# The overflow branch at the beginning of the experts, and one set of transposes ahead of two matmul groups

## The chip, the cores and the metric

The kernel runs on one core of a Trainium2 chip. The time is device microseconds (us) of one launch; lower is better. The engines of the core are TensorE (PE, with its weight loads as PEld), VectorE (DVE), ScalarE (ACT), GpSimd (POOL) and SyncE (SP). Each takes its own instructions in the order in which the program wrote them, and waits on semaphores that other engines and transfers raise.

## The reference

A chain of three stages over 1536 tokens with 512 features: a linear attention with decay in blocks, a gated layer, and a mixture of eight experts, each token going to one of them. The experts' stage, cut to what matters here (`x` is what the gated layer gave; `capacity` is 384):

```
logits = x @ w_gate
expert_idx = np.argmax(logits, axis=1)
gate_w = softmax(logits)[np.arange(N), expert_idx]
for i in range(N):                      # tokens of each expert, in order
    e = expert_idx[i]
    if counts[e] < capacity:
        disp[e, counts[e]] = x[i]
        pos[i] = counts[e]; counts[e] += 1; keep[i] = True
h = np.maximum(np.einsum('ecd,edf->ecf', disp, w1), 0.0)
y = np.einsum('ecf,efd->ecd', h, w2)
out[i] = gate_w[i] * y[expert_idx[i], pos[i]]   # where keep[i], else 0
```

## The kernel before

Matmuls take each fp32 operand as two parts, high and low (`whi`/`wlo`, `xdh`/`xdl`, `hh`/`hl`), and do three products for one (`mm3`, lines 295 to 297, and line 787). The low part is made on DVE from the original less the high part that ACT wrote.

The order of all work is written by hand (`manual_schedule`): each engine gets its instructions as the code calls for them. Background work (the loading and splitting of weights by `feed` and `run_bg`) is called in small pieces between the matmul groups. The loads go out on SP's queue (line 82, `st<-e1i` and `st<-e2i`), the gathers and scatters by row index on POOL's (lines 708 and 718).

**The stage before the experts.** `x2_half(blk, cs, hooks)` computes one block of 128 tokens and one half of the features: 8 steps `fb` of three matmuls (lines 295 to 297). `hooks` names functions to call after a step; steps are numbered 0 to 7. `half_b` computes the second half with the gate's logits and starts `route`, which finds each token's expert and its place there, and adds to `csum`, whose sum over the partitions is the number of tokens of each expert. `half_a` computes the first half, and `rows_a` writes it to `xa_d` in device memory (`rowa`, line 637, on ACT's queue). The second halves lie in `xb_d`.

**The gathers.** `gathers(e, half)` brings the rows of expert `e` from `xa_d` (half 0, tiles `xga`) or `xb_d` (half 1, tiles `xgb`) into one of two sets of buffers, in two chunks of 128 rows. `table` issues those of half 1 for experts 0 and 1. Those of half 0 can start only when the last block of `xa_d` is stored.

**The experts.** `dispatch(e, half)` transposes the gathered rows by four PE instructions (line 757), then ACT writes `xdh` (line 769) and DVE `xdl` (line 770). `mm1(e, pr, ks)` does the first layer for the pair `pr` of 128 hidden units each: for the half of the features in `ks`, `(2, 3)` being half 1 and `(0, 1)` half 0, 12 matmuls of 128x256 (line 787). At the beginning only half 1 is there, so all four pairs of expert 0 and two of expert 1 start with `(2, 3)`, six groups of 12, before half 0 of expert 0 is used. Then comes the loop over the experts, with the second layer (`mm3` with `hh`/`hl`) and the scatter of each result.

**More than 256 rows.** The main path holds two chunks, so 256 rows of an expert. `overflow()` does what lies beyond: all engines load the largest count (`cmax`, line 833) into a register and branch on it (`tc.If`, line 834). With these inputs no expert has more than 256 rows, so the body is jumped over at run time. The counts are made by one matmul of `ones` with `csum` (line 817) and a maximum on DVE (line 819). In the program the branch stands in the loop:

```
for e in range(NE):
    if nch > 2 and e == OVER:      # OVER = 7
        overflow()
```

Of the kernel before, what the change touches and what calls it, by code (L numbers as in the profile page):

```python
# [12 lines left out]
I32 = mybir.dt.int32  # L13
AF = mybir.ActivationFunctionType
ALU = mybir.AluOpType
AX = mybir.AxisListType
PSUM = bass.MemoryType.PSUM

P = 128
# [4 lines left out]
NE = 8  # L24
NC = 6
NBLK = NT // P
# [5 lines left out]
NST = 4  # L32
NW = (2, 1, 1, 1, 1, 1, 1, 1)
HOOK = 6
OVER = 7
LOADS = (1, 2, 2, 2, 2, 2, 2, 0)
TICKS = ((0, 0, 0, 0), (0, 0, 0, 1)) + ((1, 0, 0, 1),) * 6 + ((0, 0, 1, 0),)
XBW = 265
# [3 lines left out]
def tile_moe_chain(ctx, tc, cap, qk, kv, w12, w3i, woi, wgi, e1i, e2i, c32, c16, zero, out):  # L42
    nc = tc.nc
    nch = min(-(-cap // P), NBLK)
# [6 lines left out]
    def pool(name, bufs=1, **kw):  # L51
        return tc.tile_pool(name=name, bufs=bufs, reuse_waits="tile", **kw)

    const = ctx.enter_context(pool("const"))
# [9 lines left out]
    def bank():  # L64
        return ps.tile([P, 512], F32, tag="b", name="bank")
# [140 lines left out]
    def run_bg(n=1):  # L206
        for _ in range(n):
            feed.tick()
# [70 lines left out]
    csum = const.tile([P, NE], F16, name="csum")  # L279
# [14 lines left out]
    def mm3(acc, wh, wl, rh, rl, first, last):  # L294
        nc.tensor.matmul(acc, wh, rl, start=first, stop=False)  # L295
        nc.tensor.matmul(acc, wh, rh, start=False, stop=False)  # L296
        nc.tensor.matmul(acc, wl, rh, start=False, stop=last)  # L297
# [248 lines left out]
    ones = c16_sb[:, 128:256]  # L546
# [24 lines left out]
    def x2_half(blk, cs, hooks={}):  # L571
        g, tb = divmod(blk, 3)
        ts = slice(tb * P, (tb + 1) * P)
        acc = bank()[:, 0 : cs.stop - cs.start]
        for fb in range(8):
            gh, gl = gts[g, fb]
            mm3(acc, gh[:, ts], gl[:, ts], wxh[:, fb, cs], wxl[:, fb, cs], fb == 0, fb == 7)
            if fb in hooks:
                hooks[fb]()
        return acc  # L580
# [53 lines left out]
    def rows_a(blk, acc):  # L634
        row = p2.tile([P, 256], F32, tag="rowa", name="rowa")
        nc.scalar.copy(row, acc)
        nc.scalar.dma_start(xa_d[blk * P : (blk + 1) * P, :], row)
# [5 lines left out]
    def advance():  # L643
        for r in list(routing):
            if next(r, 0) == 0:
                routing.remove(r)

    def half_b(blk, hooks={}):
        acc = x2_half(blk, slice(256, 520), hooks)
        if not hooks:  # L650
            advance()
        routing.append(route(blk, acc))
        next(routing[-1])
        if not hooks:
            run_bg(1)

    def half_a(blk, hooks={}):
        acc = x2_half(blk, slice(0, 256), hooks)
        if not hooks:
            advance()  # L660
        rows_a(blk, acc)
        run_bg(1)
# [64 lines left out]
    def gathers(e, half):  # L727
        for s in range(nmain):
            gather(xg[e % 2][s][half], (xa_d, xb_d)[half], s * NE + e)
# [15 lines left out]
    def dispatch(e, half, apart=False):  # L745
        if e not in xd:
            xd[e] = (
                p3.tile([P, 4, nt], F32R, tag="xdh", name="xdh"),
                p3.tile([P, 4, nt], F32R, tag="xdl", name="xdl"),
                p3.tile([P, nmain], F32, tag="gate", name="gate"),  # L750
            )
        xh, xl, gt = xd[e]
        tp = psi.tile([P, 512], F32, tag="i", name="tp") if half else bank()
        tps = [tp[:, 0:nt], bank()[:, 0:nt] if apart else tp[:, nt : 2 * nt]]
        for kk in range(2):
            for s in range(nmain):
                nc.tensor.transpose(
                    tps[kk][:, s * P : (s + 1) * P],
                    xg[e % 2][s][half][:, kk * P : (kk + 1) * P],
                    ident,  # L760
                )
        k = 2 * half
        if apart:
            parts = [(xh[:, k + n, :], xl[:, k + n, :], tps[n]) for n in range(2)]
        else:
            tp = tp[:, 0 : 2 * nt].rearrange("p (k t) -> p k t", k=2)
            parts = [(xh[:, k : k + 2, :], xl[:, k : k + 2, :], tp)]
        for h, lo, src in parts:
            nc.scalar.copy(h, src)
            nc.vector.tensor_tensor(lo, src, h.bitcast(F32), op=ALU.subtract)  # L770
        if half:
            for s in range(nmain):
                nc.vector.tensor_copy(gt[:, s : s + 1], xg[e % 2][s][1][:, 264:265])

    def mm1(e, pr, ks):
        xh, xl, _ = xd[e]
        it = e1_it[2 * e + pr // 2]
        feed.need(it, pieces=2 * (pr % 2) + 2)
        if ks[0] == 2:
            accs[e, pr] = bank()[:, 0 : 2 * nt]  # L780
        acc = accs[e, pr]
        for m in range(2):
            hi, lo = (it.by_fb(part, (2 * pr + m) % 4) for part in (it.hi, it.lo))
            o = acc[:, m * nt : (m + 1) * nt]
            for k in ks:
                for w, x in ((hi, xl), (hi, xh), (lo, xh)):
                    nc.tensor.matmul(  # L787
                        o,
                        w[:, k, :],
                        x[:, k, :],  # L790
                        start=m == 0 and k == 2 and x is xl,
                        stop=m == 1 and k == 1 and w is lo,
                        skip_group_check=True,
                    )
        if ks[-1] == 1:
            hh = p3h.tile([P, 2, nt], F32R, tag="hh", name="hh")
            hl = p3h.tile([P, 2, nt], F32R, tag="hl", name="hl")
            acc = accs.pop((e, pr)).rearrange("p (m t) -> p m t", m=2)
            nc.scalar.activation(hh, acc, AF.Relu)  # L799
            nc.vector.scalar_tensor_tensor(  # L800
                hl, acc, 0.0, hh.bitcast(F32), op0=ALU.max, op1=ALU.subtract
            )
            hts[pr] = (hh, hl)
            it.free = pr % 2 == 1
        run_bg(2 if ks[-1] == 1 else 1)

    half_b(NBLK - 3, {8: advance})
    half_b(NBLK - 2, {4: advance})
    half_b(NBLK - 1, {4: advance})
    half_a(NBLK - 3, {3: advance, 6: advance, 7: table})  # L810
    half_a(NBLK - 2, {8: advance})
    acc = x2_half(NBLK - 1, slice(0, 256), {HOOK: lambda: dispatch(0, 1, apart=True)})
    rows_a(NBLK - 1, acc)
    gathers(0, 0)
    gathers(1, 0)
    cnt = bank()[:, 0:NE]
    nc.tensor.matmul(cnt, ones, csum, start=True, stop=True)
    cmax = const.tile([P, 1], I32, name="cmax")
    nc.vector.tensor_reduce(cmax, cnt, axis=AX.X, op=ALU.max)

    late.close()
    p3h = ctx.enter_context(pool("p3h", 6, side="right"))
    hts = {}
    for pr in range(4):
        mm1(0, pr, (2, 3))
        if pr == 1:
            dispatch(1, 1)
    mm1(1, 0, (2, 3))
    dispatch(0, 0)
    mm1(1, 1, (2, 3))  # L830

    def overflow():
        nmax = nc.values_load(cmax[0:1, 0:1], min_val=0, max_val=NT)  # L833
# [50 lines left out]
                    scatter(y, col)  # L884

    ov = ctx.enter_context(pool("ov", side="right")) if nch > 2 else None
    for e in range(NE):
        if nch > 2 and e == OVER:
            overflow()
        for pr in range(4):  # L890
            mm1(e, pr, (0, 1) if (e, pr) in accs else (2, 3, 0, 1))
        gt = xd.pop(e)[2]
        if e + 1 < NE:
            if e:
                dispatch(e + 1, 1)
            dispatch(e + 1, 0)
        if e + 2 < NE:
            gathers(e + 2, 1)
            gathers(e + 2, 0)
        for s in range(nmain):  # L900
            acc = bank()
            ss = slice(s * P, (s + 1) * P)
            for fb in range(8):
                it = e2_it[2 * e + fb // 4]
                feed.need(it)
                mm3(
                    acc,
                    hts[fb // 2][0][:, fb % 2, ss],
                    hts[fb // 2][1][:, fb % 2, ss],
                    it.view(it.hi)[:, fb % 4, :],  # L910
                    it.view(it.lo)[:, fb % 4, :],
                    fb == 0,
                    fb == 7,
                )
                it.free = s == nmain - 1 and fb % 4 == 3
                if fb % 2:
                    run_bg(1)
            y = p3.tile([P, DM], F32, tag="y", name="y", bufs=3)
            cut = DM if (e, s) != (NE - 1, nmain - 1) else DM // 2
            nc.scalar.activation(y[:, 0:cut], acc[:, 0:cut], AF.Copy, scale=gt[:, s : s + 1])  # L920
            if cut < DM:
                nc.vector.tensor_scalar(
                    y[:, cut:], acc[:, cut:], gt[:, s : s + 1], None, op0=ALU.mult
                )
            scatter(y, s * NE + e)
# [69 lines left out]
```

## Time and profile before

| | us |
|---|---|
| median of 3 runs | 513.52 |
| lowest and highest | 513.02, 513.99 |
| profiled execution | 516.84 |
| its span in the profile | 514.8 |
| mean granted clock of PE in it, share of full speed | 0.997 |

The rows of the profile are of one execution, and their times count from the start of its span. The profiled execution's own time (516.84) holds its span and 2.0 us that lie outside it. It is 3.3 us above the median of the runs that were not profiled.

### The profile page before, as it was taken

Reading aid. Unit: us, or ns where it says so; the run is one execution under the profiler, and the core shown is the slowest. Engines: PE = TensorE matmul, PEld = TensorE weight load, DVE = VectorE, ACT = ScalarE, POOL = GpSimd, SP = SyncE. Lnnn points to the kernel's source line nnn. Section 1 sums busy time; section 2 is a strip of 40 time slices with the busy share of each in tenths; the row PEclk is TensorE's granted clock in tenths of the full one; section 3 lists DMA queues with packets and bytes.
Section 4 is the critical chain, followed back from the end, with each engine's and each line's share of the span. In section 5 each row is a group of like instructions: output and inputs, shape, how many; then the busy total and the mean of one; then the engine's idle time right before and its main releaser. Section 6 shows DMA issues by size and latency. Waiting matters only on the chain. (4 is left out here: it accounts for less than half of the span.)

```text
span 514.8 us, 9557 instructions
## 1 busy us (share of the span) xinstructions
PE 498.6 (97%) x3805; PEld 468.7 (91%) x3805; DVE 264.9 (51%) x576; ACT 242.9 (47%) x485; POOL 128.7 (25%) x124
## 2 busy tenths in 40 slices
PE   8999999999999999999999998899999999999993
PEld 4888999999999999999999998789989898989892
DVE  5998875668332223222332563468383746547420
ACT  2697997789311221122112424457464746546310
POOL 4365664545100000000020005405414040410101
PEclk9999999999999999999999999999999999999998
DMA  8999565557801000100010224486666666574200
GB/s 325 413 410 375 155 227 204 189 187 247 320 26 41 1 0 23 43 1 0 23 43 0 88 69 157 162 299 219 214 213 211 224 224 228 177 250 171 83 2 34
DMA packets 24529, 80.80 MB, mean 157 GB/s; under 512 B 3642, under 2 KB 5692, under 8 KB 24480
## 3 DMA queue, kind: packets, MB, share of 16 engines
q1 hardware_dynamic: 18976, 70.35, 38.4%
q0 software_dynamic: 3344, 7.85, 4.8%
q10 hardware_dynamic: 2160, 1.94, 1.1%
q8 instruction: 32, 0.52, 0.4%
q14 instruction: 17, 0.14, 0.1%
HBM read 74.84 MB, written 10.54 MB: 166 GB/s over the span
## 5 line engine op out<-in xcount | busy, mean ns | idle before, releaser
L97 DVE TENSOR_TENSOR wlo<-st,whi 128x512 fp32r<-128x512 f32 x128 | 82.0, 684 | 16.7 <-ACT whi L95 16.7
L295 PE MATMUL bank<-xtl,whi 128*128 128x384 f32 x256 | 87.1, 340 | 0.0
L297 PE MATMUL bank<-xth,wlo 128*128 128x384 f32 x256 | 86.4, 337 | 0.0
L296 PE MATMUL bank<-xth,whi 128*128 128x384 f32 x256 | 85.8, 335 | 0.0
L95 ACT CAST whi<-st 128x512 fp32r<-128x512 f32 x128 | 73.1, 621 | 16.2 <-PE bank L297 10.7
L787 PE MATMUL bank<-xdl,whi 128*128 128x256 f32 x256 | 72.6, 283 | 4.7 <-issue 2.5
L787 PE MATMUL bank<-xdh,whi 128*128 128x256 f32 x256 | 72.2, 282 | 0.0
L787 PE MATMUL bank<-xdh,wlo 128*128 128x256 f32 x256 | 72.1, 282 | 0.0
L143 POOL TENSOR_TENSOR wlo<-t,whi 128x512 fp32r<-128x512 f32 x40 | 51.9, 1298 | 52.1 <-ACT whi L142 46.5
L295 PE MATMUL bank<-wxl,gh 128*128 128x264 f32 (+1 forms) x192 | 55.9, 291 | 0.0
L296 PE MATMUL bank<-wxh,gh 128*128 128x264 f32 (+1 forms) x192 | 54.1, 282 | 0.0
L297 PE MATMUL bank<-wxh,gl 128*128 128x264 f32 (+1 forms) x192 | 54.1, 282 | 0.0
L787 PEld LDWEIGHTS bank<-xdl,whi 128*128 128x128 f32 x256 | 48.4, 189 | 5.6 <-issue 2.7
L564 DVE TENSOR_TENSOR a_sb<-bank,a_sb 128x384 f32<-128x384 f32 x32 | 17.8, 557 | 66.9 <-PE bank L297 66.3
L295 PE MATMUL bank<-wlo,hh 128*128 128x512 f32 x128 | 51.1, 399 | 0.0
L297 PE MATMUL bank<-whi,hl 128*128 128x512 f32 x128 | 50.4, 394 | 0.0
L718 POOL DMA_INDIRECT out_dram<-y,idx x16 | 16.6, 1038 | 134.2 <-ACT y L920 101.1
L296 PE MATMUL bank<-whi,hh 128*128 128x512 f32 x128 | 50.0, 391 | 0.0
L800 DVE SCALAR_TENSOR_TENSOR hl<-bank,hh 128x512 fp32r<-128x512 f32 x32 | 22.1, 690 | 53.3 <-ACT hh L799 45.5
L787 PEld LDWEIGHTS bank<-xdh,whi 128*128 128x128 f32 x256 | 48.3, 189 | 0.3
L787 PEld LDWEIGHTS bank<-xdh,wlo 128*128 128x128 f32 x256 | 48.4, 189 | 0.0
L295 PEld LDWEIGHTS bank<-xtl,whi 128*128 128x128 f32 x256 | 48.1, 188 | 0.0
(109 smaller groups left out, 1006.1 us busy)
## 6 DMA issues: line engine op xcount, KB each, us to landing
st<-e1i SPq DMA_DIRECT2D x32, 512.0 KB
st<-e2i SPq DMA_DIRECT2D x32, 512.0 KB
st<-w3i SPq DMA_DIRECT2D x16, 512.0 KB
st<-w SPq DMA_DIRECT2D x16, 512.0 KB
tqk<-qk SPq DMA_DIRECT2D x8, 768.0 KB
tkv<-kv SPq DMA_DIRECT2D x8, 768.0 KB
st<-woi SPq DMA_DIRECT2D x8, 512.0 KB
out_dram<-zero SPq DMA_DIRECT2D x1, 3072.0 KB
```

The source lines that it names most:

```text
L95: nc.scalar.copy(h, s)
L97: nc.vector.tensor_tensor(lo, s, h.bitcast(F32), op=ALU.subtract)
L143: nc.gpsimd.tensor_tensor(lo, t, h.bitcast(F32), op=ALU.subtract)
L295: nc.tensor.matmul(acc, wh, rl, start=first, stop=False)
L296: nc.tensor.matmul(acc, wh, rh, start=False, stop=False)
L297: nc.tensor.matmul(acc, wl, rh, start=False, stop=last)
L564: nc.vector.tensor_tensor(a_sb, acc, a_sb, op=ALU.mult)
L718: nc.gpsimd.indirect_dma_start(out=out, out_offset=bass.IndirectOffsetOnAxis(ap=idx[:, col : col + 1], axis=0), in_=src, in_offset=None, b ...
L787: nc.tensor.matmul(o, w[:, k, :], x[:, k, :], start=m == 0 and k == 2 and x is xl, stop=m == 1 and k == 1 and w is lo, skip_group_check=True,)
L800: nc.vector.scalar_tensor_tensor(hl, acc, 0.0, hh.bitcast(F32), op0=ALU.max, op1=ALU.subtract)
```

## The change

`count`, the matmul and the maximum that give `cmax`, becomes a function and is called as a hook after step 2 of the first half of block 10 (it stood behind the gathers of `xga`; the hook `{8: advance}` that it replaces is never called, since the steps end at 7). `overflow()` is called once, before the gathers of `xga` and the first expert matmuls, and no longer in the loop. `dispatch(0, 0)`, the transposes of expert 0's first half, stands ahead of `mm1(1, 0, (2, 3))` and no longer behind it. Nothing else is changed; from there on, line numbers of the change are 1 less in the functions above and 7 to 9 less in `count` and `overflow`.

```
-OVER = 7
...
+    cmax = const.tile([P, 1], I32, name="cmax")
+
+    def count():
+        cnt = bank()[:, 0:NE]
+        nc.tensor.matmul(cnt, ones, csum, start=True, stop=True)
+        nc.vector.tensor_reduce(cmax, cnt, axis=AX.X, op=ALU.max)
+
...
-    half_a(NBLK - 2, {8: advance})
+    half_a(NBLK - 2, {2: count})
     acc = x2_half(NBLK - 1, slice(0, 256), {HOOK: lambda: dispatch(0, 1, apart=True)})
     rows_a(NBLK - 1, acc)
-    gathers(0, 0)
-    gathers(1, 0)
-    cnt = bank()[:, 0:NE]
-    nc.tensor.matmul(cnt, ones, csum, start=True, stop=True)
-    cmax = const.tile([P, 1], I32, name="cmax")
-    nc.vector.tensor_reduce(cmax, cnt, axis=AX.X, op=ALU.max)
-
     late.close()
     p3h = ctx.enter_context(pool("p3h", 6, side="right"))
-    hts = {}
-    for pr in range(4):
-        mm1(0, pr, (2, 3))
-        if pr == 1:
-            dispatch(1, 1)
-    mm1(1, 0, (2, 3))
-    dispatch(0, 0)
-    mm1(1, 1, (2, 3))
...
     ov = ctx.enter_context(pool("ov", side="right")) if nch > 2 else None
+    if nch > 2:
+        overflow()
+    gathers(0, 0)
+    gathers(1, 0)
+    hts = {}
+    for pr in range(4):
+        mm1(0, pr, (2, 3))
+        if pr == 1:
+            dispatch(1, 1)
+    dispatch(0, 0)
+    mm1(1, 0, (2, 3))
+    mm1(1, 1, (2, 3))
     for e in range(NE):
-        if nch > 2 and e == OVER:
-            overflow()
         for pr in range(4):
             mm1(e, pr, (0, 1) if (e, pr) in accs else (2, 3, 0, 1))
```

How the instructions stand on the engines, first PE between the stage before and the first expert matmul. Before:

```order
L295 MATMUL bank<-wxl,gh 128x256
L296 MATMUL bank<-wxh,gh 128x256
L297 MATMUL bank<-wxh,gl 128x256
L817 LDWEIGHTS c_sb
L817 MATMUL bank<-csum,c_sb 128x8
L787 MATMUL bank<-xdl,whi 128x256 [waits DVE_49]
L787 MATMUL bank<-xdh,whi 128x256 [waits Activation_49]
```

The count matmul is the one of line 817 (`c_sb` holds `ones`); the expert's first matmul waits for DVE's `xdl`. The same place of PE in the change:

```order
L294 MATMUL bank<-wxl,gh 128x256
L295 MATMUL bank<-wxh,gh 128x256
L296 MATMUL bank<-wxh,gl 128x256
L824 TENSOR_LOAD cmax [waits DVE_49]
L825 COMPARE_AND_BRANCH
...
L825 UNCONDITIONAL_BRANCH
L825 UNCONDITIONAL_BRANCH [waits PE_49]
L786 MATMUL bank<-xdl,whi 128x256 [waits DVE_49,PE_49]
```

In the place of the count matmul stand the load of `cmax` and the branch, whose jumped-over body is left out here; the wait of the expert's first matmul for PE itself is new. The count matmul stands further up, in the stream of block 10.

PE at the transposes of expert 0's first half (`xga00` and `xga01` are their two chunks; `bank_3947` and `bank_3971` are the results of `mm1(1, 0)` and `mm1(1, 1)`, 12 matmuls each). Before:

```order
L787 MATMUL bank_3947<-xdh_3901,whi_3771 128x256
L787 MATMUL bank_3947<-xdh_3901,wlo_3772 128x256
L757 MATMUL bank_3964<-c32_sb_79,xga00_3532 128x128
L757 MATMUL bank_3964<-c32_sb_79,xga01_3534 128x128
L757 MATMUL bank_3964<-c32_sb_79,xga00_3532 128x128
L757 MATMUL bank_3964<-c32_sb_79,xga01_3534 128x128
L787 MATMUL bank_3971<-xdl_3902,whi_3771 128x256
L787 MATMUL bank_3971<-xdh_3901,whi_3771 128x256
```

One group of expert 1 stands ahead of the four transposes and one behind. In the change (`bank_4619` is the result of `mm1(0, 3)`, `bank_4641` that of `mm1(1, 0)`):

```order
L786 MATMUL bank_4619<-xdh_3830,whi_3463 128x256
L786 MATMUL bank_4619<-xdh_3830,wlo_3464 128x256
L756 MATMUL bank_4634<-c32_sb_79,xga00_3532 128x128
L756 MATMUL bank_4634<-c32_sb_79,xga01_3534 128x128
L756 MATMUL bank_4634<-c32_sb_79,xga00_3532 128x128
L756 MATMUL bank_4634<-c32_sb_79,xga01_3534 128x128
L786 MATMUL bank_4641<-xdl_4589,whi_3772 128x256
L786 MATMUL bank_4641<-xdh_4588,whi_3772 128x256
```

The transposes moved up by one group of 12, so that both groups of expert 1, 24 matmuls, stand behind them.

POOL at the gathers of the first halves. Before:

```order
L708 DMA xgb11_3539<-xb_d_78,idx_81 128x265 [waits Pool_49]
L708 DMA xga00_3532<-xa_d_77,idx_81 128x256 [waits DMAHW5_49,DMAHW3_49,DMAHW6_49,DMAHW2_49,DMAHW7_49,DMAHW1_49,DMAHW0_49]
L708 DMA xga01_3534<-xa_d_77,idx_81 128x256
L708 DMA xga10_3536<-xa_d_77,idx_81 128x256
L708 DMA xga11_3538<-xa_d_77,idx_81 128x256
```

The first `xga` gather follows the last `xgb` gather at once and waits for the stores of `xa_d` alone. In the change:

```order
L707 DMA xgb11_3539<-xb_d_78,idx_81 128x265 [waits Pool_49]
L824 TENSOR_LOAD cmax_3548 [waits DVE_49]
L825 COMPARE_AND_BRANCH
...
L825 UNCONDITIONAL_BRANCH
L825 ISA [waits DMASW4_49,DMASW5_49,DMASW3_49,DMASW6_49,DMASW2_49,DMASW7_49,DMASW1_49,DMASW0_49]
L825 UNCONDITIONAL_BRANCH
L707 DMA xga00_3532<-xa_d_77,idx_81 128x256 [waits DMAHW3_49,DMAHW5_49,DMAHW2_49,DMAHW6_49,DMAHW1_49,DMAHW7_49,DMAHW0_49,DMASW7_49]
L707 DMA xga01_3534<-xa_d_77,idx_81 128x256 [waits DMASW0_49]
```

Between them stand now the load of `cmax`, the branch and an instruction that waits for all gathers under way (`DMASW`) and updates their counters. On SP the branch stands likewise between two loads of weights (`st<-e2i`), with a wait for all loads and stores under way behind it.

## Rows read from the trace of the kernel before

**Rows 1.** The page, part 1: busy us, share of the span, instructions.

```profile
PE 498.6 (97%) x3805; PEld 468.7 (91%) x3805; DVE 264.9 (51%) x576; ACT 242.9 (47%) x485; POOL 128.7 (25%) x124
```

**Rows 2.** Waits of PE, 300 to 515: what for, us in total, times, longest.

```profile
PE bank L787 <- issue: 2.5, 1, 2.5
PE bank L787 <- DVE xdl L770: 1.3, 1, 1.3
PE bank L787 <- PEq L834: 0.8, 1, 0.8
```

**Rows 3.** Timeline, PE, expert 7: start, us, what, [idle before, releaser].

```profile
482.59 0.39 PE L296 MATMUL bank<-whi,hh 128*128 128x512 f32 x1
482.82 0.39 PE L297 MATMUL bank<-whi,hl 128*128 128x512 f32 x1
484.01 0.36 PE L787 MATMUL bank<-xdl,whi 128*128 128x256 f32 x1 [0.80 <-PEq L834]
```

**Rows 4.** Instructions of line 834: shortest/median/longest ns, first and last start.

```profile
L834 PEldq COMPARE_BRANCH  x1: 4148/4148/4148, 479.5 to 479.5; - x1
...
L834 POOLq INC_SWDGE_SEM  x1: 1332/1332/1332, 487.8 to 487.8; - x1
```

**Rows 5.** Timeline, PE, the experts' beginning.

```profile
314.25 0.28 PE L297 MATMUL bank<-wxh,gl 128*128 128x256 f32 x1
314.37 0.18 PE L817 MATMUL bank<-csum,c_sb 128*128 128x8 f16 x1
315.89 0.39 PE L787 MATMUL bank<-xdl,whi 128*128 128x256 f32 x1 [1.34 <-DVE xdl L770]
```

**Rows 6.** Timeline, PE, transposes of experts 1 and 0, and the matmuls behind.

```profile
318.86 0.60 PE L757 MATMUL tp<-c_sb,xgb 128*128 128x128 f32 x4
319.21 0.37 PE L787 MATMUL bank<-xdl,whi 128*128 128x256 f32 x1
...
323.59 0.60 PE L757 MATMUL bank<-c_sb,xga 128*128 128x128 f32 x4
...
328.12 0.39 PE L787 MATMUL bank<-xdl,whi 128*128 128x256 f32 x1 [2.51 <-issue]
```

**Rows 7.** Timeline, ACT: the copies of these transposes.

```profile
319.50 0.59 ACT L769 CAST xdh<-tp 128x512 fp32r<-128x512 f32 x1 [2.02 <-PE tp L757]
...
326.75 0.59 ACT L769 CAST xdh<-bank 128x512 fp32r<-128x512 f32 x1 [5.11 <-remote]
```

**Rows 8.** Timeline, DVE: the low part of expert 0's first half.

```profile
327.37 0.69 DVE L770 TENSOR_TENSOR xdl<-bank,xdh 128x512 fp32r<-128x512 f32 x1 [4.64 <-issue]
```

**Rows 9.** Timeline, POOL: the gathers' issues.

```profile
313.20 1.00 POOL L708 DMA_INDIRECT xgb<-xb_d,idx  x1 [0.31 <-issue]
317.93 1.00 POOL L708 DMA_INDIRECT xga<-xa_d,idx  x1 [3.73 <-DMA xa_d<-rowa]
319.23 1.00 POOL L708 DMA_INDIRECT xga<-xa_d,idx  x1 [0.31 <-issue]
...
326.95 1.00 POOL L708 DMA_INDIRECT xga<-xa_d,idx  x1 [1.35 <-remote]
```

**Rows 10.** Timeline, PE: small matmuls between large ones.

```profile
303.40 0.28 PE L297 MATMUL bank<-wxh,gl 128*128 128x264 f32 x1
303.52 0.23 PE L624 MATMUL tabs<-val,sel 128*128 128x8 f16 x3
303.61 0.17 PE L607 MATMUL bank<-oh,c_sb 128*128 128x8 f16 x1
...
303.86 0.29 PE L296 MATMUL bank<-wxh,gh 128*128 128x264 f32 x1
```

**Rows 11.** The chain that ended last: start, us, what.

```profile
461.85 2.62 DMA out_dram<-y,idx
...
484.21 4.80 DMA out_dram<-y,idx
```

**Rows 12.** Timeline, SP: the loads' issues.

```profile
317.03 4.89 SPq L82 DMA_DIRECT2D st<-e2i  x2
```

**Rows 13.** Windows of 1 us: PE, PEld, DVE, ACT, POOL busy, clock, DMA share, GB/s.

```profile
318.00:319.00 1.00, 1.00 (x11) 1.00 (x10) 0.00 (x0) 0.00 (x0) 0.92 (x1) 1.00 0.93 332
321.00:322.00 1.00, 1.00 (x11) 1.00 (x10) 1.00 (x2) 0.64 (x2) 0.69 (x2) 1.00 0.07 12
```

## The prediction

> **What bounds the kernel now.** I read the page first: TensorE (PE) is busy for 97% of the span and no other engine for more than 51% [rows 1], so only time in which PE stands still can be won, and time added to its stream is lost. The waits of PE in the second half of the span came next. There are three [rows 2]: 2.5 us and 1.3 us before matmuls of line 787, and 0.8 us behind the branch of line 834. The reader is to see that this change touches all three. Then I read the timeline around each.
>
> The 0.8 us lie at expert 7. The last matmul before the branch starts at 482.82 and the first behind it at 484.01; the step between two such matmuls is 0.23 [rows 3]. PE's compare stands for 4.15 us [rows 4]: PE's sequencer comes to it far ahead of the array and then waits until the array has run empty. So a branch costs PE its own restart, not a long wait, wherever it stands.
>
> The 1.3 us lie at the experts' beginning: the last matmul of the stage before ends at 314.25 + 0.28 = 314.53, the small count matmul follows in the gap, and the first expert matmul waits until 315.89 for `xdl` [rows 5], which DVE and ACT make from the transposes of expert 0's second half.
>
> The 2.5 us lie behind the transposes of expert 0's first half (`xga`). They start at 323.59 and by their rows end at 324.19; 12 matmuls of expert 1 follow; then PE stands until 328.12 [rows 6]. ACT copies the transposes only at 326.75, after an idle time whose releaser is "remote" [rows 7], DVE follows at 327.37 [rows 8], and POOL's next gather into the same buffer, which waits for the same transposes, starts at 326.95 [rows 9]. At expert 1's second half ACT began at 319.50, 0.04 behind the transposes' end at 319.46 [rows 6, 7]. So here ACT came 2.56 us later than the rows of PE explain.
>
> **The change, part by part.**
>
> *Branch taken out at expert 7.* PE's step there falls from 484.01 - 482.82 = 1.19 to 0.23: 0.96 us less. From expert 0 on PE is without a gap but for these waits, so this reaches the end. POOL's barrier behind that branch (its counter update took 1.33 us, rows 4) lay under matmuls there and gives nothing back.
>
> *Branch put in at the beginning.* On PE it needs 0.80 of idle time behind the last matmul's end [rows 3]: 314.53 + 0.80 = 315.33, before 315.89. The wait for `xdl` covers it; ACT and DVE write `xdh` and `xdl` ahead of their own branches. Cost 0; without that cover it would be 0.8 us. Behind it on ACT and DVE stand weight splits, which had 2.0 us of idle time before the next transposes came [rows 7].
>
> *The count matmul* moves from the gap into a dense stream. From 303.40 to 303.86 PE did two large steps and five such small matmuls; large steps are 0.12 (36 matmuls between 319.21 and 323.59, rows 6), so five cost 0.46 - 0.24 = 0.22 [rows 10], one 0.04. It delays everything to the next wait by 0.05. Bounds 0 and 0.1.
>
> *POOL's queue.* The four gathers of the first halves now stand behind the branch, where POOL waits for every gather still under way and then updates its counters, 1.33 us. The last gather ahead of it starts at 313.20 [rows 9]. How long a gather takes to land no row shows; the indirect writes of the end, nearest in kind, took 2.62 to 4.80 us [rows 11]. POOL would be free between 313.20 + 2.62 + 1.33 = 317.15 and 319.33. The first gather starts at 317.93 anyway, since it waits for the store of `rowa`. I take 0, because no load is under way then; the bound is 1.4.
>
> *SP's queue.* SP waits for all transfers in flight behind its branch, the store of `rowa` among them, which landed by 317.93. So the load that went out at 317.03 [rows 12] goes about 0.9 later and runs into the gathers: the DMA engines were 0.93 busy at 318 to 319, with the load, and 0.07 at 321 to 322 [rows 13]. I put 0.3 of it on the gathers (bounds 0 and 0.9).
>
> *Transposes moved ahead of one matmul pair.* PE comes to them 12 matmuls earlier: 323.59 - 12 x 0.122 + 0.05 = 322.18. They need expert 0's second gather, issued at 319.23; with 2.62 to 4.80 it lands between 321.85 and 324.03. Since the DMA engines were all but idle from 321 on, I take 322.4, and with the load 322.7. The four transposes take 0.35 (318.86 to 319.21), the 24 matmuls of both pairs 2.92: PE could go on at 325.97. The chain beside it: transposes' end 323.30, ACT 0.04 later, then 1.37 from ACT's start to PE's (326.75 to 328.12): 324.71, well before. So the 2.5 us go, unless ACT's late start goes along. 328.12 - 325.97 = 2.15 us less.
>
> The bounds of this term: landing at 321.85 leaves no wait and resumes at 325.45 (2.67 less); landing at 324.03 + 0.9 resumes at 328.2, which is worth nothing.
>
> What let ACT go at 326.75 is the open point. [...]
>
> **Sum.** -0.96 - 2.15 = -3.11 us. The profiled execution took 516.84 us (span 514.8 and what lies around it), so such a one would take 513.73; it is 3.3 us above the median of the runs, and the difference is what I carry over: 513.52 - 3.11 = 510.4 us.
>
> [...]
>
> **Rivals.**
>
> *The delay goes along.* ACT starts 2.56 us after the transposes' end again: 323.30 + 2.56 + 1.37 = 327.23, 0.89 before 328.12. With the branch -1.85: 511.7. For it: it is a property of these transposes in this trace. Against it: those of 318.86 do not have it.
>
> *The release is tied to something else,* which comes at 326.75 whatever PE does. Then only the branch pays: -0.96, 512.6, no change by the measure below.
>
> *The 2.5 us are not there in runs without a profile.* For it: the profiled run is 3.3 us longer than the median. Then before would resume at 324.19 + 0.04 + 1.37 = 325.60, and the change at 325.97 is 0.37 worse there: 0.37 - 0.96 = -0.6, 512.9.
>
> *Slower: the gathers become the bound.* The moved transposes have 0.2 us of slack toward the gather's landing L instead of 1.2, and PE resumes at L + 0.35 + 2.92. POOL's wait for the earlier gathers and its 1.33 us push L directly. Against before with its 2.5 us, the change loses over 0.2% only from L = 328.12 + 0.96 + 1.03 - 3.27 = 326.84; without these 2.5 us from 324.32, which is inside the bounds 324.03 + 1.4. At 325.43 PE resumes at 328.70, 3.10 later than 325.60, less 0.96: 515.7.
>
> **How the numbers follow.** No change can be told within about 0.2%, 1.03 us. Chances: forecast 0.42, the delay goes along 0.10, release elsewhere 0.13, not there without a profile 0.15, gathers as the bound 0.20. Faster: 0.42 + 0.10 and 0.02 of the unsure cases, 0.54; same 0.26; slower 0.20. The predicted time is 510.4; alone it has 509.8 to 512.6 from its bounds. The range leaves out most of the slower case: 509.7 to 514.4.
>
> **What would show it.** PE's row of the branch gone at expert 7 and a step of 0.23 us there; one PE wait of 1.2 to 1.5 us before the first expert matmul, put down to `xdl` and not to the branch; POOL's counter update ending before the first `xga` gather starts near 317.9; `xga` transposes near 322.7; ACT's copy within 0.1 us of their end; no PE wait before the 24 matmuls' successor. Wrong would be: an `xga` gather starting behind 318.5, a PE wait at the transposes of over 1 us, or again a "remote" release of ACT.

## The result and the profile after

The change is slower. It took 519.75 us (median of 4 runs, 518.57 to 520.67) where before took 513.44; the ratio is 1.0125, 95% interval 1.0113 to 1.0137. Forecast were 510.4 us and a range up to 514.4. Run again beside the experiments, it took 519.02 us and before 517.14: 1.0041, interval 1.0025 to 1.0057. The change's own time is the same in both, within a microsecond; before's is not, and a part of that is accounted for below. Both intervals lie above 1, so the change is slower. By how much is less sure: of before in the first measurement only one execution has its span and granted clock on record, as all others here have, and it took 516.84 us, like the later ones. So 0.4% is the better founded size of the loss.

In the profiled executions the span goes from 514.8 to 518.9 us, and PE is still the engine that is always busy (page, part 1):

```profile
PE 499.9 (96%) x3805; PEld 470.9 (91%) x3805; DVE 265.2 (51%) x576; ACT 243.2 (47%) x485; POOL 128.0 (25%) x124
```

The waits of PE from 300 us to the end, to be held against [rows 2]: the 1.3 us for `xdl` and the 0.8 us at expert 7 are gone, a wait of 3.8 us behind the branch has come, and a wait of 2.5 us put down to "issue" is there again.

```profile
PE bank L786 <- PEq L825: 3.8, 1, 3.8
PE bank L786 <- issue: 2.5, 1, 2.5
```

But this 2.5 us is another one. The timeline of PE at the branch shows it four matmuls behind the first expert matmul, in the middle of one group, where [rows 6] had it 12 matmuls behind the transposes of `xga`:

```profile
314.75 0.28 PE L296 MATMUL bank<-wxh,gl 128*128 128x256 f32 x1
318.83 0.36 PE L786 MATMUL bank<-xdl,whi 128*128 128x256 f32 x1 [3.81 <-PEq L825]
...
319.27 0.28 PE L786 MATMUL bank<-xdl,whi 128*128 128x256 f32 x1
322.05 0.58 PE L786 MATMUL bank<-xdh,whi 128*128 128x256 f32 x1 [2.51 <-issue]
```

What the engines did in the branch's line (shortest/median/longest ns, first and last start):

```profile
L825 SPq EVENT_SEMAPHORE  x8: 17/17/17, 318.3 to 318.8; - x8
...
L825 PEldq COMPARE_BRANCH  x1: 3792/3792/3792, 314.7 to 314.7; - x1
...
L825 POOLq INC_SWDGE_SEM  x1: 496/496/496, 316.8 to 316.8; - x1
```

PE's compare starts at 314.7, when the array has one matmul left, and lasts 3.79 us. In [rows 4] it lasted 4.15 us, but there it started at 479.5, 3.3 us ahead of the last matmul's start. So the compare has changed little; the cover in front of it is gone. Two rows of PE's sequencer show why it had no lead here: a semaphore at the transposes of `xgb`, three matmuls ahead, and then the load of `cmax` into a register.

```profile
L756 PEldq EVENT_SEMAPHORE  x1: 51/51/51, 313.9 to 313.9; - x1
```

```profile
L824 PEldq TENSOR_LOAD <-cmax x1: 487/487/487, 314.1 to 314.1; - x1
```

Beside both waits stands a load on the queue of instructions (transfers from 316 to 317 us, then from 319 to 320: packets, MB, share):

```profile
q8 instruction: 1, 0.02, 5.7%
```

```profile
q8 instruction: 1, 0.02, 8.0%
```

Such a load did not by itself make PE wait: in the first profile of before the same queue has 8 of them from 340 to 480 us (`q8 instruction: 8, 0.13, 0.4%`), and PE had no wait between 330 and 482 us.

Then the clock: in windows of 5 us the granted clock falls to 0.50 from 320 us on. In the 5 us ahead PE had worked for 0.74 us (columns as in [rows 13]).

```profile
315.00:320.00 5.00, 0.74 (x5) 0.54 (x4) 2.15 (x6) 1.57 (x4) 0.99 (x1) 0.98 0.19 54
320.00:325.00 5.00, 2.95 (x14) 2.95 (x14) 0.00 (x0) 0.00 (x0) 3.79 (x4) 0.50 0.52 176
325.00:330.00 5.00, 5.00 (x38) 5.00 (x38) 2.01 (x5) 1.62 (x3) 1.20 (x2) 0.83 0.12 32
```

And the places that let the loss be counted, PE again: the transposes of expert 1's second half, those of `xga`, the first matmul behind the two groups that follow, and expert 7's first matmul, now without a wait.

```profile
326.49 0.69 PE L756 MATMUL tp<-c_sb,xgb 128*128 128x128 f32 x4
...
329.88 0.60 PE L756 MATMUL bank<-c_sb,xga 128*128 128x128 f32 x4
...
333.17 0.28 PE L786 MATMUL bank<-xdl,whi 128*128 128x256 f32 x1
...
487.80 0.40 PE L296 MATMUL bank<-whi,hl 128*128 128x512 f32 x1
488.03 0.28 PE L786 MATMUL bank<-xdl,whi 128*128 128x256 f32 x1
```

The account of the profiled executions: the first expert matmul is 318.83 - 315.89 = 2.94 us later than in [rows 5]. Four matmuls on, the second wait: 322.05 - 319.27 less a step of 0.12 is 2.66. From there to 326.49 PE did 20 matmuls in 4.44 us, which take 2.44 at the step of 0.122 that [rows 6] had from 319.21 to 323.59: 2.0 for the clock of 0.50. Sum 7.60; the transposes of expert 1 stand 326.49 - 318.86 = 7.63 later. Behind the two groups it is 333.17 - 328.12 = 5.05: the old wait of 2.5 us is not there. At expert 7 it is 488.03 - 484.01 = 4.02, since the step there is now 0.23. The span grew by 4.1.

### The profile page after: what moved, and what is told of

It is laid out like the page before. It is cut to its first block, busy times and chain, and to the rows that moved or that the text cites. A ratio compares the mean times of both kernels' runs of the same rounds, so it can differ in the third digit from the quotient of the medians.

```text
span 518.9 us, 9556 instructions
## 1 busy us (share of the span) xinstructions
PE 499.9 (96%) x3805; PEld 470.9 (91%) x3805; DVE 265.2 (51%) x576; ACT 243.2 (47%) x485; POOL 128.0 (25%) x124
## 5 line engine op out<-in xcount | busy, mean ns | idle before, releaser
L786 PE MATMUL bank<-xdl,whi 128*128 128x256 f32 x256 | 73.2, 286 | 3.8 <-PEq L825 3.8
L786 PE MATMUL bank<-xdh,whi 128*128 128x256 f32 x256 | 73.3, 286 | 2.5 <-issue 2.5
L786 PE MATMUL bank<-xdh,wlo 128*128 128x256 f32 x256 | 73.1, 286 | 0.0
L786 PEld LDWEIGHTS bank<-xdl,whi 128*128 128x128 f32 x256 | 49.3, 193 | 4.3 <-PEq L825 4.0
L786 PEld LDWEIGHTS bank<-xdh,whi 128*128 128x128 f32 x256 | 49.2, 192 | 3.0 <-issue 2.7
L786 PEld LDWEIGHTS bank<-xdh,wlo 128*128 128x128 f32 x256 | 49.4, 193 | 0.0
```

The lines of the kernel that those rows point to most:

```text
L786: nc.tensor.matmul(o, w[:, k, :], x[:, k, :], start=m == 0 and k == 2 and x is xl, stop=m == 1 and k == 1 and w is lo, skip_group_check=True,)
```

## The experiments

Theory A: PE waits at the branch for the program's code behind the long body that is jumped over, and again for the next piece of it. Theory B: PE is held until SP and POOL are through with their waits at the branch (SP's counts ended at 318.8, PE went on at 318.83). C: the moved transposes cost the time. Ratios are to before, timed on the same chip in the same stretch. Expectations in us were written for a before of 513.5; it stood at 517 to 518 there, so the ratios are to be compared.

**The branch alone.** `dispatch(0, 0)` goes back between the groups:

```
-    dispatch(0, 0)
     mm1(1, 0, (2, 3))
+    dispatch(0, 0)
     mm1(1, 1, (2, 3))
```

> The change without the move of the transposes: branch and count at the beginning, the transposes of expert 0's first half between the two matmul groups of expert 1 as before. Theory A (PE's branch waits for the program code behind the long body that is jumped over: 3.81 us before the first expert matmul and 2.51 us four matmuls later in the profile of the change, then about 2 us at the lower granted clock) expects nearly the time of the change, 519 to 520 us, with the same two PE waits. Theory B (PE is held at the branch until SP and POOL are through their own waits there, which ended at 318.3 to 318.8 while PE went on at 318.83) expects the same. Rival C (the loss comes from the moved transposes, which would then stand in PE's way) expects about 512.6 us, before less the 0.96 us of the branch at expert 7.

519.98 us, 1.0051 (1.0033 to 1.0069). The waits of PE:

```profile
PE bank L786 <- PEq L825: 3.8, 1, 3.8
...
PE bank L786 <- issue: 1.7, 1, 1.7
```

The whole loss is there without the moved transposes. C falls.

**The transposes alone.** The same two lines moved in the kernel before; the branch stays at expert 7.

> The kernel before with only the transposes of expert 0's first half moved ahead of both matmul groups of expert 1; the branch stays at expert 7. If the 2.51 us wait of the profiled run of before is there in every run and goes (the forecast's term), 511.0 to 511.6 us. If that wait is not there in runs without a profile, 513.4 to 513.9 us, same or up to 0.4 us more. Rival C expects a loss of several us. Theories A and B say nothing on this one beyond that the branch keeps its price at expert 7.

516.15 us, 0.9974 (0.9959 to 0.9988): a gain of 1.35 us, between the two expectations. The wait behind the transposes is gone, smaller ones have come a little later, with no releaser shown (waits of PE from 300 us on):

```profile
PE bank L787 <- issue: 1.4, 2, 1.0
PE bank L787 <- DVE xdl L770: 1.4, 1, 1.4
PE bank L787 <- PEq L834: 0.7, 1, 0.7
```

**A shorter body.** Only the number of experts in the body that is jumped over changes; the branch and the register loads stay. What SP waits for behind the branch changes with it: eight counts (EVENT_SEMAPHORE in line 825) with two, four or eight experts, four with one.

```
-            for e in range(NE):
+            for e in range(1):      # in two further runs 4 and 2
                 for s in range(2, nch):
```

> The change with the body behind the branch cut from eight experts to one (rows above 256 of experts 1 to 7 are left out; no expert has any here, and the body is jumped over in either case). The branch, its place, its loads of the count and the waits of SP and POOL stay. Theory A: PE's compare ends at once or within 1 us, no wait of 2.5 us behind it and no fall of the granted clock; 519.6 less about 7 us, 512 to 513 us. Theory B: PE still goes on only when SP is through, near 318.5 us; the time stays at 518 to 520 us. Rival C: no change, 519 to 520 us.

515.89 us, 0.9969 (0.9955 to 0.9982). PE's compare in line 825:

```profile
L825 PEldq COMPARE_BRANCH  x1: 353/353/353, 315.4 to 315.4; - x1
```

> The change with the body cut from eight experts to four (rows above 256 of experts 4 to 7 are left out; there are none). Theory A in its simple form: the jump still leads past the code that PE's queue has loaded, one block of it has to come, so PE's compare takes 3 to 4 us as with eight experts and the granted clock falls again: 518 to 520 us. If PE's price grows with the length of the body instead (all of it is brought in), the compare takes about half, 2 us, and the time lies near 516.5 us.

516.68 us, 0.9983 (0.997 to 0.9996). The compare, and the waits of PE from 200 us on:

```profile
L825 PEldq COMPARE_BRANCH  x1: 3489/3489/3489, 315.0 to 315.0; - x1
```

```profile
PE bank L786 <- PEq L825: 3.4, 1, 3.4
```

> The change with a body of two experts (rows above 256 of experts 2 to 7 are left out; there are none). One expert took 353 ns in the compare and 0.9969 of before. By the simple form of theory A it is all or nothing: either 0.4 us and 0.997, if the target is within what was loaded, or 3 to 4 us and 1.003 to 1.005. By a price that grows with length about 0.8 us and 0.9975.

516.15 us, 0.9972 (0.996 to 0.9984).

```profile
L825 PEldq COMPARE_BRANCH  x1: 352/352/352, 314.8 to 314.8; - x1
```

So the compare took 0.35 us over one or two experts and 3.5 to 3.8 over four or eight: a step, not a slope. That it changed with the length of the body that is jumped over is shown; that it is a wait for code is the author's reading of the length and of the loads beside it, and was not shown.

The run with one expert does not decide on B, since SP was through by 312.2 us there. The one with two does: SP's counts ended as late as in the change, and PE's first expert matmul was released at 317.2, by DVE.

```profile
L825 SPq EVENT_SEMAPHORE  x8: 17/17/17, 318.4 to 318.9; - x8
...
L825 DVEq EVENT_SEMAPHORE  x1: 21/21/21, 317.2 to 317.2; - x1
```

So B falls. With four experts the second wait of 2.5 us is missing, and the ratio is 0.9983 against the change's 1.0041; the fall of the clock is there in part (0.87 and 0.79 in the windows from 315 and from 320 us on). What brings the second wait was not shown.

The two short bodies leave another wait in the place of the old one for `xdl`. With one expert PE's waits were:

```profile
PE bank L786 <- DVEq L825: 2.1, 1, 2.1
PE bank L786 <- issue: 0.8, 2, 0.4
```

The first expert matmul waited for DVE's count behind DVE's own branch, not for `xdl` alone: 2.1 us where [rows 2] had 1.3. With two experts it was 2.3 us, and the mean granted clock of that profile was 0.991; with one expert it was 0.997, and 1.00 in the same windows.

**No branch.** `overflow()` is taken out of the change.

> The change without the branch and its body (rows above 256 are left out; there are none here). It is the floor for any place of the branch. Theories A and B: before less the 0.96 us at expert 7, 512.0 to 512.8 us, and 2 us less if the 2.51 us wait of before was real and goes with the moved transposes. Rival C: 517 us or more. The granted clock stays at full speed by A and B.

514.91 us, 0.9955 (0.9939 to 0.9972). Taken as ratios to 513.5, A expects 0.997 to 0.999 without the wait of 2.5 us and 0.993 to 0.995 with it; the measured one lies between, far from C's. Against the transposes alone, which keep the branch at expert 7, that is 516.15 - 514.91 = 1.24 us for the branch there.

**The change again.** Nothing edited.

> The change itself, once more, beside the experiments of this call. In the first measurement it stood at 1.0125 of before (513.4 us there); where the branch alone was timed, before stood at 517.6 us and the branch alone at 1.0051. If the PE waits of 3.8 and 2.5 us and the low clock behind them are what the change costs, its own time is the same wherever it is run (519 to 520.5 us), and what differs is before: then 1.003 to 1.006 here if before stands near 517.5 us, and 1.012 if it stands near 513.5 us.

519.02 us, 1.0041 (1.0025 to 1.0057); before stood at 517.14. As expected, its PE waits were 3.5 and 2.4 us.

**The branch behind dense matmuls.** The change with the branch at the beginning of expert 3:

```
     for e in range(NE):
+        if nch > 2 and e == 3:
+            overflow()
```

> The change with the branch, its full body of eight experts and its early count, at the beginning of expert 3 in the loop, behind 48 dense matmuls of 128x512. Theory A: PE's compare takes about 4 us here too, but PE's sequencer stands there some 3.3 us ahead of the array, so PE's wait is 0.7 to 0.9 us as at expert 7, without a fall of the clock: 0.997 to 0.998 of before, the time of the moved transposes alone (0.9974). If the early place in the program and not the missing lead made it dear, the wait is nearer 3.8 us. Theory B: PE held until SP has waited for its loads under way, 3 to 6 us.

516.14 us, 0.9991 (0.9977 to 1.0006). Line 825 again:

```profile
L825 SPq EVENT_SEMAPHORE  x8: 17/17/17, 388.9 to 392.4; - x8
...
L825 PEldq COMPARE_BRANCH  x1: 5152/5152/5152, 384.2 to 384.2; - x1
...
L825 PEldq EVENT_SEMAPHORE  x1: 51/51/51, 389.4 to 389.4; - x1
```

PE's compare ended at 389.4, and the next matmul was released by what PE put right behind it (`PE bank L786 <- PEq L825: 1.8, 1, 1.8`), not by SP, which was through at 392.4: B falls a second time. The compare was longer than expected, 5.15 us, and PE's wait 1.8 us rather than 0.7 to 0.9; the cover was there (5.15 less 1.8, some 3.3 us of the compare that did not show), the size was missed.

**The branch at the end.** Once ahead of the last scatter, once behind it:

```
+            if nch > 2 and (e, s) == (NE - 1, nmain - 1):
+                overflow()
             scatter(y, s * NE + e)
```

> The change with the branch moved to the end, between the last scaling of y and the last scatter. PE has no matmul behind it, so theory A lets its wait for code (3.8 us from where its sequencer comes to the branch, about 3.3 us ahead of the last matmul's start at expert 7) lie beside the last scaling and the scatter's landing. A price of 0.5 to 1.0 us stays, since the scatter waits for DVE's count behind DVE's branch (register load about 0.5 us, branch and count 0.2 to 0.3 us). Against the version without a branch (0.9955 of before) 0.9965 to 0.9985. Theory B (all engines held until SP and POOL are through) would put POOL's wait for the scatter before it on the path as well: it landed by then, so it costs nothing more here; B does not differ.

515.61 us, 0.9978 (0.9966 to 0.9991), as expected: PE's compare took 4.19 us there too, with nothing behind it on PE.

> The change with the branch moved behind the last scatter, so that nothing but the end of the program stands behind it. POOL waits there for the last scatter's landing, as the end does anyway, and then updates its counters (0.5 us at the change's place, 1.33 us at expert 7). Against the version without a branch: 0.5 to 1.4 us more, 0.9965 to 0.998 of before. If the update is not on the path, 0.9955.

518.08 us, 1.0028 (1.0015 to 1.0041): a miss. POOL's part behind the last scatter (EVENT_SEMAPHORE holds its wait for the scatter's landing):

```profile
L825 POOLq EVENT_SEMAPHORE  x4: 17/43/2300, 505.8 to 508.3; - x4
...
L825 POOLq INC_SWDGE_SEM  x1: 1380/1380/1380, 508.4 to 508.4; - x1
```

The wait of 2.30 us for the landing and the update of 1.38 us stand one behind the other, and then comes the program's own end; it costs 2.5 us more than the place one scatter earlier.

**The short body at expert 7.** The kernel before with `range(1)` in the body.

> The kernel before, branch at expert 7, with the body cut to one expert (rows above 256 of experts 1 to 7 are left out; there are none). Theory A: PE's compare falls from 4.1 us to 0.4, and since PE's sequencer stands over 3 us ahead there, PE's wait of 0.7 to 0.8 us falls to the register's and counts' share, 0 to 0.4 us: 0.5 to 0.8 us less than before, 0.9985. If the wait at expert 7 is PE's own restart and not its code (the forecast's reading), 0.8 us stay and the time is that of before.

517.45 us, 1.0003 (0.9989 to 1.0016). The compare fell to 0.23 us and PE's wait from 0.8 to 0.3, as A expects; the time does not show these 0.5 us, since its interval is wider than they are.

**Before, profiled once more.**

> The kernel before, profiled once more, for one look at what its time is made of where it stands near 517 us and not 513.5: whether the wait of 2.5 us behind the transposes of expert 0's first half is there, where the granted clock falls, and whether anything ahead of 300 us differs.

517.85 us. Waits of PE from 200 us on, and two windows (columns as in [rows 13]):

```profile
PE bank L787 <- issue: 2.5, 1, 2.5
PE bank L787 <- DVE xdl L770: 1.2, 1, 1.2
PE bank L787 <- PEq L834: 0.8, 1, 0.8
```

```profile
325.00:330.00 5.00, 2.53 (x18) 2.33 (x18) 1.29 (x2) 1.23 (x3) 2.73 (x3) 0.92 0.39 137
330.00:335.00 5.00, 5.00 (x34) 5.00 (x33) 3.83 (x7) 4.06 (x8) 0.00 (x0) 0.73 0.30 109
```

The wait of 2.5 us is there as in [rows 6], and here the granted clock falls behind it. In the first profile of before it did not:

```profile
325.00:330.00 5.00, 2.49 (x21) 2.29 (x20) 1.29 (x2) 1.25 (x3) 2.88 (x3) 1.00 0.43 155
330.00:335.00 5.00, 5.00 (x42) 4.92 (x41) 4.52 (x8) 5.00 (x11) 0.00 (x0) 1.00 0.34 123
```

So this wait can cost more than its length. How often it does can be estimated from the mean granted clock of before's executions beside the experiments: 40 have 0.996 or 0.997, as the first profile has, and 61 have 0.991 to 0.994, as this one has. In each of the four series the second kind is longer, by 1.4 to 1.7 us on average. A kernel that takes this wait away can gain both.

**Later gathers.** In the first profile of before, POOL issues the gathers for expert 2 just where ACT's copy comes late, between the transposes at 323.59 and ACT's start at 326.75 (timeline of POOL):

```profile
323.31 1.00 POOL L708 DMA_INDIRECT xgb<-xb_d,idx  x1 [0.30 <-issue]
324.61 1.00 POOL L708 DMA_INDIRECT xgb<-xb_d,idx  x1 [0.30 <-issue]
```

They move behind the first scatter of expert 0, with nothing else changed:

```
-        if e + 2 < NE:
+        if 0 < e < NE - 2:
             gathers(e + 2, 1)
             gathers(e + 2, 0)
...
             scatter(y, s * NE + e)
+            if (e, s) == (0, 0):
+                gathers(2, 1)
+                gathers(2, 0)
```

> The kernel before, with only the gathers for expert 2 moved behind the first scatter of expert 0 (they were issued from 323.3 us on, now near 340). If these gathers hold back PE's count, ACT's start follows the transposes of expert 0's first half within 0.1 us, PE's wait there falls from 2.5 us to 1.4 or less (ACT's start to PE's took 1.37), and the granted clock does not fall behind it: 0.994 to 0.998 of before. If they have no part in it, the wait of 2.5 us and the time of before stay.

514.18 us, 0.9928 (0.9913 to 0.9943). PE's waits from 300 us on, the transposes of `xga` on PE, and ACT's copy of them:

```profile
PE bank L787 <- DVE xdl L770: 1.1, 1, 1.1
PE bank L787 <- PEq L834: 0.8, 1, 0.8
```

```profile
324.03 0.60 PE L757 MATMUL bank<-c_sb,xga 128*128 128x128 f32 x4
```

```profile
324.66 0.59 ACT L769 CAST xdh<-bank 128x512 fp32r<-128x512 f32 x1 [2.58 <-PE bank L757]
```

ACT starts 0.03 us behind the transposes' end, and the wait of 2.5 us is gone, with the transposes where before has them. Of before's 17 executions in this series 13 are of the kind with the lower clock; the other four took 516.8 us on average, 2.6 us more than this kernel, which is the wait's length. With the two that follow it is the fastest of the kernels here that compute the whole.

> The moved transposes alone (0.9974 of before) with the gathers for expert 2 moved behind the first scatter of expert 0. If the gathers hold back PE's count, the waits of 0.97 and 0.43 us behind 328 us go as well: 0.994 to 0.996. If not, 0.9974.

514.32 us, 0.9928 (0.991 to 0.9945): no gain of the moved transposes is to be seen beside the later gathers.

> The branch ahead of the last scatter (0.9978 of before), the moved transposes and the later gathers for expert 2 together; it computes all that the change computes. If the gathers hold back PE's count 0.994 to 0.996, with the branch's price at the end (about 0.7 us) still in it; if not 0.9978.

514.61 us, 0.9943 (0.9924 to 0.9962), no better than the later gathers alone. ACT's copy is not on time here, though the gathers for expert 2 are away: the transposes ended at 323.59, and it started 0.72 us behind, beside the gathers for expert 1. PE had no wait from it.

```profile
324.31 0.59 ACT L768 CAST xdh<-bank 128x512 fp32r<-128x512 f32 x1 [2.66 <-PE bank L756]
```

## Why the prediction was wrong

**The step that failed** is "a branch costs PE its own restart, not a long wait, wherever it stands", and with it "Cost 0" for the branch put in at the beginning. The row was read rightly, 4.15 us of compare and 0.80 us of idle time, but the 4.15 us were taken for the array running empty. They are PE's own: 0.35 us with a body of one or two experts, 3.5 us and more with four or eight. At expert 7 the compare starts 3.3 us ahead of the last matmul's start, so 0.8 us show. At the new place PE's sequencer comes to it with one matmul left: it has a semaphore at the transposes three matmuls ahead, at 313.9, and then a register load of 0.49 us. (That the semaphore holds it for the gather that these transposes read is likely, not shown.) So nearly all of the compare shows, a wait of 3.81 us, and the first expert matmul starts 2.94 us later than before.

The step lies between two and four experts. By the program the body has 44 matmuls and as many weight loads an expert (4 transposes, 32 and 8 matmuls), so PE had 176 of these instructions to jump over where the compare took 0.35 us, and 352 where it took 3.49. Why the step lies there was not shown.

**What followed from it.** A second wait of 2.66 us and 2.0 us at the clock of 0.50, neither of which had a term. The forecast asked what the branch waits for and not what PE does behind a stop.

**The branch taken out at expert 7**, -0.96 us: right, with a step of 0.23 us there and 1.24 us between the runs with and without it. Its reason was not: with the short body most of the 0.8 us went.

**The cover by `xdl`.** It was not whole either. DVE writes `xdl` ahead of its branch, but the matmul waits for a count that DVE raises behind it; with a short body, where this can be seen, the wait was 2.1 and 2.3 us instead of 1.3. So the cost was not 0 even without PE's long compare.

**POOL's and SP's queues.** POOL's update took 0.50 us and was done before 317.9, as forecast. The first `xga` gather still went out at 319.00, over a microsecond later, for a reason that the forecast did not have; the timeline of POOL names it:

```profile
319.00 0.99 POOL L707 DMA_INDIRECT xga<-xa_d,idx  x1 [4.27 <-SPq L825]
```

It waits for counts that SP puts right behind its own wait, until 318.8. PE stood still at that time and had no wait at the transposes of `xga`, so no loss came of it.

**The moved transposes**, -2.15 us: right in sign, 1.35 us alone (0.6 to 2.1 by the interval). Of these some 0.9 us are before's fall of the clock, by an estimate from its series (13 of 25 executions, 1.66 us each); against the other 12, whose median is 516.6, the gain is 0.45 us. In the change ACT followed the transposes by 0.03 us, as forecast, but by luck: the stops had put the transposes at 329.88, behind the issue of expert 2's gathers, the last of which ahead of them ended at 326.50. Moved alone they ended at 323.24, ACT came 0.89 us later, and PE had two shorter waits.

The forecast had four ways for ACT's late start: it stays away, goes along, is tied to something else, or is a matter of the profile. The gathers for expert 2, whose issue starts at 323.31, bring about most of it: with them moved ACT follows the transposes by 0.03 us and the 12 matmuls cover the rest. They are not all of it, as the 0.72 us of the last run show. Why ACT starts late beside these gathers is open.

**The slower rival** had a chance of 0.20 and a range to 515.7 us, by the gathers of `xga`. The time went its way, past its end, by another mechanism.

**The base of the sum.** The forecast took its 3.11 us off 513.52 and carried 3.3 us over as the difference between profiled and other executions. The later executions of before took 514.7 to 518.9 us, around the 516.84 of the profiled one, so that difference is not borne out; from 516.84 the sum would have been 513.73. The change's 519 lies above either. (The lower end of the forecast's own span comes out of its terms as 509.9, not 509.8.)

**Left open:** why before took 513.4 us in the first measurement and 517 to 518 in the later ones. The wait of 2.5 us with and without a fall of the clock makes steps of 1.4 to 1.7 us within the later ones, but even the shorter kind took 515.8 to 516.8 us on average there; no profile with 513.4 us is at hand. And the count matmul's 0.05 us were not measured by themselves.

## What to carry to other kernels

A branch's price was not the 0.8 us of idle time that the profile of before showed at it: read the compare's own length, and how far ahead of the array the sequencer stood when it began. The jump over the long unrolled body here wanted a shorter body (0.23 to 0.35 us of compare over one or two experts), or a place where the sequencer stands as far ahead of the array as the compare takes, 3.5 to 5.2 us over four or eight; with 3.3 us ahead 0.8 us showed at expert 7 and 1.8 at expert 3. A place that no matmul follows was no cheaper here (0.9978 of before, against 0.9974 at expert 7 with the same transposes). And where a release comes late without a cause in its own engine, look at which gathers or scatters are under way: moving those (0.9928 of before) was worth more here than moving the work that waited (0.9974).

## What was unexpected of the hardware

The compare of a branch on PE took 0.23 to 0.35 us over a body of one or two experts, and 3.5 to 5.2 us over four or eight, while the other engines took 0.05 to 0.07 us for theirs. ACT's copy of the transposes started 2.56 us after their end by the rows with gathers being issued beside it, and 0.03 us after it with the gathers for expert 2 moved away (0.72 us in one run even so). And a stop of PE of 2.5 us was followed by a lower granted clock in one profile of the same kernel (0.73 in the window from 330 us on) and not in the other (1.00).
